# First two token tiles of a two-layer transformer kernel: centred only, with the deviation applied to the logits

## The chip, the cores and the metric

The kernel runs on one core of one Trainium2 chip. A core has a TensorE for matrix products (PE in the profile, with PEld for its weight loads), a VectorE (DVE), a ScalarE (ACT) and a GpSimd (POOL), each with its own in-order instruction queue, and a SyncE (SP) whose queue issues the DMAs here. The metric is the device time of one execution in microseconds. Four executions of the kernel before took 1617.11 to 1617.64 us, median 1617.24.

## The reference

The input x has 2048 tokens of 1024 numbers in bf16. Two kinds of layer alternate, two of each, all with the same weights:

```python
x = x + _A_ref(_layernorm(x, axis=-1), A_wqkv, A_wo)
x = x + _B_ref(_layernorm(x, axis=-1), B_w1, B_w3, B_w2)
x = x + _A_ref(_layernorm(x, axis=-1), A_wqkv, A_wo)
x = x + _B_ref(_layernorm(x, axis=-1), B_w1, B_w3, B_w2)
```

`_layernorm` is (x - mean) / sqrt(var + 1e-5) without gain or bias. `_A_ref` is an attention of 32 heads of 32 numbers over a window: token s looks at the eight tokens s, s-2, ..., s-14. The logit of a head is q · k * 32^-0.5, positions before the first token are masked, a softmax over the eight follows, and the weighted sum of v goes through `wo`. `_B_ref` is a gated feed-forward: silu(x w1) * (x w3), 3584 wide, times w2.

Since a layer norm's division is one number per token, and q is linear in the normalised token, the division can as well be made on the token's logits: with q computed from (x - mean) alone, q · k has to be multiplied by 1/sqrt(var + 1e-5) of the query's token before mask and softmax.

## The kernel before, in words

**Tiling.** A token tile is 128 tokens (x_sb[0] to x_sb[15], all kept in SBUF), a chunk is four tiles (512 tokens). `ln` makes the layer norm of one chunk: per tile bn_stats on two halves, aggregate, root on ScalarE (L313), reciprocal (L315), subtract and multiply (L320) into a bf16 tile xn[j], and then a transpose into xnT, where the model dimension lies on the partitions in eight blocks of 128 (index kk). There are two xnT buffers, used by the stages in turn. For all chunks but the first the transpose is a DMA issued by SP (L253).

**Stages.** A q stage computes q, k and v of one chunk (24 groups of eight 128x512 products, L355), copies each result out of PSUM on ScalarE (L407; for chunk 0 k and v also straight into kT and vT, L410), and spills pairs of blocks to DRAM (qkv_d). An attention step works on half a chunk: load qT, kT, vT, multiply and add on VectorE (L259), transpose the partial sums so that tokens lie on partitions, sum to the logits L, mask, softmax (exp on ScalarE, L519), weighted sum, and the projection with `wo` on TensorE (32 products), added to x on VectorE (L545). A feed-forward stage runs two chains of products, silu on ScalarE (L568), the product on VectorE (L570), and a second run of products added to x (L600).

**What sets the order.** The kernel writes its operations down with reads, writes and an estimated duration. `Program.place` then plans one order for each engine's queue from these estimates, with classes as priorities (smaller goes first) and, for TensorE, lanes: lane 2 (the start's transposes) before lane 1 (the projections) before lane 0. The queues are executed in this order on the chip; nothing is reordered there. So a change at the start also shifts, by a group of products here and there, what stands where later on. A DMA is issued only after the DMA eight places before it has landed (the waits on eight completion semaphores in turn).

**The first stage.** `q_first` (L422) is special, because nothing can be computed until x has come in. SP issues x tiles 0 and 1 (256 KB each), then the q weights as eight rows kk of 256 KB, then x tiles 2 and 3 (L423 to L425), then the k weights in two pieces of 1 MB, x of chunk 1, and so on. Meanwhile TensorE multiplies a tile of zeros (`warm`, NWARM = 12 products of 128x512, L278). `ln(0, first=True)` handles tile after tile: statistics, root, apply, eight TensorE transposes into one PSUM bank (L334) and one ScalarE copy of 128x1024 into xnT (L339). The q products of chunk 0 (L438) have 128 columns, one token tile at a time, 8 output blocks m for each kk, in the order tile 0 kk 0 to 4, tile 1 kk 0 to 4, both kk 5 to 7, tile 2, tile 3:

```python
order = [(0, 0, 5), (1, 0, 5), (0, 5, 8), (1, 5, 8), (2, 0, 8), (3, 0, 8)]
```

Their results go by ScalarE (L444) to hT[:, 0:8], a buffer that the feed-forward stages need only later, and from there to DRAM. Then come k and v of chunk 0 (L355 from `q_tile`), and the attention of chunk 0 begins when q has been read back.

Of the kernel before, what the change touches and what calls it, by code (L numbers as in the profile page):

```python
# [154 lines left out]
def kernel(  # L155
# [24 lines left out]
    scale = float(Dh) ** -0.5  # L180
    EPS = 1e-5
    NSLOT = 6
    NWARM = 12

    xin = A_x[0].rearrange("(n p) d -> p n d", p=P)
    xout = out[0].rearrange("(n p) d -> p n d", p=P)
# [11 lines left out]
    def alloc(name, shape, dt=BF16):  # L198
        return sb.tile(shape, dt, name=name)
# [29 lines left out]
    rs = alloc("rs", [P, NE], FP32)  # L229
    rsb = alloc("rsb", [P, NE])  # L230
    An = alloc("An", [P, W, NE])
    oT = [alloc(f"oT{i}", [P, KT, TCH]) for i in range(2)]
    qkv_d = [[dram.tile([D, S], BF16, name=f"qkv_d{l}_{i}") for i in range(3)] for l in range(2)]
    bank = [pp.tile([P, 512], FP32, name=f"bank{i}") for i in range(8)]
# [6 lines left out]
    def t1(n):  # L241
        return 0.15 + n / 960.0

    def dve(dur, emit, reads, writes, cls=2, **kw):
        return pr.add("DVE", dur, emit, reads, writes, cls, **kw)
# [4 lines left out]
    def dma(kb, dst, src, reads, writes, cls=3, transpose=False):  # L250
        def emit(op):
            if transpose:
                nc.sync.dma_start_transpose(dst, src)  # L253
            else:
                nc.sync.dma_start(dst, src)
        return pr.add("SP", 0.45, emit, reads, writes, cls, size=kb * 1024)
# [28 lines left out]
    def take_slot():  # L285
        i = n_slot[0] % NSLOT
        n_slot[0] += 1
        return i

    def load_x(c, j0=0, j1=TPC, after=()):  # L290
        for j in range(j0, j1):
            n = c * TPC + j
            dma(256, x_sb[n][:], xin[:, n, :], after, [("x", n, 0), ("x", n, 1)], 0 if c == 0 else 3)
# [3 lines left out]
    def ln(c, first=False):  # L297
        s = stage_no[0]
        b, q = s % 2, s % 4
        xb = xnT[b]  # L300

        def stats(j):
            n = c * TPC + j
            pri = j - 9 if first else 1
            for hh in range(2):
                dve(0.67, lambda _, hh=hh: nc.vector.bn_stats(st[q][:, j, hh, :],  # L306
                                                              x_sb[n][:, hh * 512:(hh + 1) * 512]),
                    [("x", n, hh)], [("st", q, j, hh)], pri)
            dve(0.2, lambda _: nc.vector.bn_aggr(mv[q][:, j, :], st[q][:, j, :, :]),  # L309
                [("st", q, j, 0), ("st", q, j, 1)], [("mv", q, j)], pri)  # L310

        def root(j0, j1):
            act(0.3, lambda _: nc.scalar.activation(sd[q][:, j0:j1], mv[q][:, j0:j1, 1], ACTF.Sqrt, bias=epst[:]),  # L313
                [("mv", q, j) for j in range(j0, j1)] + ["eps"], [("sd", q, j) for j in range(j0, j1)], j0 - 9 if first else 0, table="sqrt")
            dve(0.16, lambda _: nc.vector.reciprocal(rstd[q][:, j0:j1], sd[q][:, j0:j1]),  # L315
                [("sd", q, j) for j in range(j0, j1)], [("rstd", q, j) for j in range(j0, j1)], j0 - 9 if first else 0)

        def apply(j):
            n = c * TPC + j
            dve(0.5, lambda _: nc.vector.tensor_scalar(xn[j][:], x_sb[n][:], mv[q][:, j, 0:1], rstd[q][:, j:j + 1],  # L320
                                                       op0=ALU.subtract, op1=ALU.mult),
                [("x", n, 0), ("x", n, 1), ("mv", q, j), ("rstd", q, j)], [("xn", j)], j - 9 if first else 1)

        if first:
            for j in range(TPC):
                stats(j)
                root(j, j + 1)
                apply(j)
                a = Acc()

                def tr(op, j=j, a=a):
                    pt = bank[a.bank][:].bitcast(BF16)
                    for kk in range(KT):
                        nc.tensor.transpose(pt[:, kk * P:(kk + 1) * P], xn[j][:, kk * P:(kk + 1) * P], ident[:])  # L334
                tro = pr.add("PE", 0.5, tr, [("xn", j), "ident"], [], takes=[a], lag=0.17, lane=2)

                def ev(op, j=j, a=a):
                    pt = bank[a.bank][:].bitcast(BF16)
                    nc.scalar.copy(xb[:, :, j * P:(j + 1) * P], pt.rearrange("p (k t) -> p k t", k=KT))  # L339
                evac(act, 1.0, ev, tro, [], [("xnT", b, j)], a)  # L340
            return b
        for j in range(TPC):
            stats(j)
        root(0, TPC)
        for j in range(TPC):
            apply(j)
            dma(256, xb[:, :, j * P:(j + 1) * P], xn[j][:], [("xn", j)], [("xnT", b, j)], 0, transpose=True)
        return b
# [10 lines left out]
    def evac(add, dur, emit, last_mm, reads, writes, a, cls=0, **kw):  # L359
        op = add(dur, emit, reads, writes, cls, gives=[a], **kw)  # L360
        op.deps.add(last_mm)
        return op

    wslots = {}

    def q_weights(which, split):
        ids = [take_slot(), take_slot()]
        for h, i in enumerate(ids):
            if split != "c":
                v = slot[i][:].rearrange("p (k c) -> p k c", k=4)  # L370
                for k in range(0, 4, 1 if split == "k" else 4):
                    n = 1 if split == "k" else 4
                    dma(256 * n, v[:, k:k + n, :], wqkv_v[:, 4 * h + k:4 * h + k + n, which * D:(which + 1) * D], [],
                        [("w", i, k + z) for z in range(n)], 0 if split == "k" else 3)
            else:
                v = slot[i][:].rearrange("p (k c) -> p k c", k=KT)
                dma(1024, v, wqkv_v[:, :, which * D + h * 512:which * D + (h + 1) * 512], [],
                    [("w", i, k) for k in range(4)], 3)
        return ids, split
# [35 lines left out]
    def q_stage(l, c):  # L415
# [3 lines left out]
            q_tile(l, c, which, ws, b)  # L419
        stage_no[0] += 1  # L420

    def q_first():  # L422
        load_x(0, 0, 2)  # L423
        wslots[0] = q_weights(0, "k")
        load_x(0, 2, 4)  # L425
        b = ln(0, first=True)
        accs = {}
        order = [(0, 0, 5), (1, 0, 5), (0, 5, 8), (1, 5, 8), (2, 0, 8), (3, 0, 8)]
        for j, k0, k1 in order:
            if j not in accs:  # L430
                accs[j] = [Acc(), Acc()]
            pa = accs[j]
            for kk in range(k0, k1):
                lk = [q_lhs(wslots[0], kk, m) for m in range(KT)]

                def emit(op, kk=kk, j=j, pa=pa, lk=lk):
                    for m in range(KT):
                        nc.tensor.matmul(bank[pa[m // 4].bank][:, (m % 4) * P:(m % 4 + 1) * P], lhsT=lk[m][0],  # L438
                                         rhs=xnT[b][:, kk, j * P:(j + 1) * P], start=(kk == 0 and m % 4 == 0),
                                         stop=(kk == KT - 1), skip_group_check=True)  # L440
                op = pr.add("PE", 8 * 0.056, emit, [lk[0][1], ("xnT", b, j)], [], takes=pa, lag=0.17)
            if k1 == KT:
                for g in range(2):
                    evac(act, 0.59, lambda _, a=pa[g], g=g, j=j: nc.scalar.copy(  # L444
                        hT[:, 4 * g:4 * g + 4, j * P:(j + 1) * P],
                        bank[a.bank][:].rearrange("p (m t) -> p m t", m=4)), op, [],
                        [("hT", 4 * g + m, j) for m in range(4)], pa[g])
        for m0 in range(0, KT, 2):
            dma(256, spill_view(0, 0, m0, 0), hT[:, m0:m0 + 2, :],
                [("hT", m, j) for m in (m0, m0 + 1) for j in range(TPC)], [("d", 0, 0, 0, m0)], 1)  # L450
        wslots[1] = q_weights(1, "s")
        load_x(1)
        load_x(2, 0, 2)
        wslots[2] = q_weights(2, "s")
        load_x(2, 2, 4, [("hT", 7, TPC - 1)])
        load_x(3, 0, 4, [("hT", 7, TPC - 1)])
        for which, key, tile_ in ((1, "kT", kT), (2, "vT", vT)):
            dve(0.11, lambda _, tile_=tile_: nc.vector.memset(tile_[:, :, 0:HALO], 0.0), [], [(key, "h")], 1)
            q_tile(0, 0, which, wslots[which], b, (key, tile_))
        dma(2048, wo[:], wo_v, [("d", 0, 2, 0, 6)], ["wo"], 3)  # L460
        stage_no[0] += 1
# [25 lines left out]
    def t_stage(l, half):  # L487
# [22 lines left out]
                                                psm[:].rearrange("p w s -> p (w s)")), allA, ["pB"])  # L510
        dve(1.22, vtt(l2, psmT[:, :, 0:2], psmT[:, :, 2:4], ALU.add), ["pB"], [l2k])
        dve(t1(512), vtt(L.rearrange("p w e -> p (w e)"), l2[:, :, 0], l2[:, :, 1], ALU.add), [l2k], [Lk])
        if tok0 == 0:
            dve(t1(64), vtt(L[:, :, 0:8], L[:, :, 0:8], maskT[:], ALU.add), [Lk, "mask"], [Lk])
        dve(t1(256), vtt(m4, L[:, 0:4, :], L[:, 4:8, :], ALU.max), [Lk], [Lk])
# [157 lines left out]
```

## Time and profile before

| | us |
|---|---|
| the profiled execution, whole | 1617.13 |
| its span (first to last instruction) | 1615.4 |
| TensorE busy | 1602.9 |
| VectorE busy | 1120.5 |
| ScalarE busy | 329.0 |
| GpSimd busy | 1.9 |
| HBM traffic over the span | 166 GB/s |

The profile is of one execution. Its page has the busy time of each engine, the span in 40 slices, the DMA queues, the chain of work that ended last, the costliest groups of instructions by line, and the DMA issues. The trace can be asked for more: a timeline (start and duration of each instruction or run of equal instructions, with the idle time before it and what ended it in brackets), and for a DMA the time from issue to landing. Line numbers in the profile are those of the kernel. A TensorE group's duration includes the tail of its last product, so groups that follow each other overlap by some 0.2 us. SPq rows are the times that SP spends on issuing, not the transfers. In a row `out<-in` names the tiles, with buffer numbers left out; `x8` is the number of instructions run together.

### The profile page before, as it was taken

How to read it: one execution, taken by the hardware profiler on the slowest of the kernel's cores; microseconds unless marked ns; L12 is line 12 of the kernel's file. 1: busy time of each engine (PE TensorE's matmuls, PEld its weight loads, DVE VectorE, ACT ScalarE, POOL GpSimd, SP SyncE). 2: the span in 40 equal slices, each digit the busy share in tenths (PEclk: the TensorE clock that was granted, in tenths of full speed). 3: DMA queues.
4: the chain of work that ended last, by engine and by line, in shares of the span. 5: the costliest groups of instructions: out<-in, count | busy, mean ns of one | idle time of the engine just before them, and what ended most of it. 6: DMA issues, size and time to landing. Idle time of an engine off the chain costs nothing.

```text
span 1615.4 us, 19247 instructions
## 1 busy us (share of the span) xinstructions
PE 1602.9 (99%) x7569; PEld 764.7 (47%) x7716; DVE 1120.5 (69%) x1900; ACT 329.0 (20%) x519; POOL 1.9 (0%) x12
## 2 busy tenths in 40 slices
PE   9999999999999999999999999999999999999999
PEld 7555544444444444444444444444444444444444
DVE  5898888889889888888898728884298832211211
ACT  4423322021211222113211032110321101101110
POOL 0000000000000000000000000000000000000000
PEclk9999999999999999999999999999999999999999
DMA  9734755385548663858545487465873464454451
GB/s 313 216 106 140 234 170 158 121 225 177 171 132 242 198 199 125 219 166 247 176 142 157 162 245 224 127 169 178 251 226 118 156 183 156 144 173 153 156 165 44
DMA packets 347818, 285.30 MB, mean 177 GB/s; under 512 B 70096, under 2 KB 342480, under 8 KB 347600
## 3 DMA queue, kind: packets, MB, share of 16 engines
q1 hardware_dynamic: 347728, 284.07, 58.4%
q8 instruction: 60, 0.98, 0.3%
q14 instruction: 30, 0.25, 0.0%
HBM read 238.94 MB, written 29.36 MB: 166 GB/s over the span
## 4 chain that ended last, share of the span: by engine, by line
PE 99%; issue 0%; DVE 0%; DMA 0%; ACT 0%
PE bank L355 98%; PE bank L438 1%; DMA x<-in_A_x_dram 0%; DVE st L306 0%; PE bank L334 0%; ACT xnT L339 0%; DVE xn L320 0%; DVE x L600 0%; DVE mv L309 0%; DVE rstd L315 0%
## 5 line engine op out<-in xcount | busy, mean ns | idle before, releaser
L355 PE MATMUL bank<-xnT,slot 128*128 128x512 bf16 x4955 | 1088.7, 379 | 5.3
L355 PEld LDWEIGHTS <-slot 128*128 128x128 bf16 x5056 | 518.0, 102 | 573.0
L355 PE MATMUL bank<-slot,hT 128*128 128x512 bf16 (+2 forms) x1812 | 387.3, 372 | 1.9
L570 DVE TENSOR_TENSOR hT<-sg,bank 128x512 bf16<-128x512 bf16 x224 | 153.5, 685 | 212.4 <-PE bank L355 196.0
L259 DVE TENSOR_TENSOR scr<-scr 128x1024 bf16<-128x1024 bf16 (+3 forms) x576 | 293.7, 540 | 2.1
L355 PEld LDWEIGHTS <-hT 128*128 128x128 bf16 x1848 | 178.6, 98 | 208.7
L568 ACT ACTIVATE sg<-bank 128x512 bf16<-128x512 f32 x224 | 133.7, 597 | 654.1 <-PE bank L355 611.1
L259 DVE TENSOR_TENSOR scr<-qT,kT 128x2048 bf16<-128x2048 bf16 x128 | 154.3, 1222 | 70.3 <-DMA kT<-qkv_d 70.3
L407 ACT CAST sgt<-bank 128x512 bf16<-128x512 f32 x184 | 107.5, 585 | 290.2 <-PE bank L355 276.6
L259 DVE TENSOR_TENSOR scr<-pA,vT 128x2048 bf16<-128x2048 bf16 x128 | 152.9, 1222 | 0.4
L600 DVE TENSOR_TENSOR x<-x,bank 128x512 bf16<-128x512 bf16 (+1 forms) x66 | 43.7, 670 | 122.6 <-PE bank L355 122.4
L355 PE MATMUL bank<-wo,oT 128*128 128x512 bf16 x502 | 112.6, 379 | 0.5
L306 DVE BATCH_NORM_STATS2 st<-x 128x6 f32<-128x512 bf16 x128 | 84.3, 682 | 18.6 <-DMA x<-in_A_x_dram 18.1
L355 PEld LDWEIGHTS <-oT 128*128 128x128 bf16 x512 | 50.1, 98 | 60.3
L545 DVE TENSOR_TENSOR x<-x,bank 128x512 bf16<-128x512 bf16 x64 | 43.9, 686 | 35.9 <-PE bank L355 34.4
L313 ACT ACTIVATE sd<-mv,epst 128x4 f32<-128x4 f32 (+1 forms) x19 | 5.7, 298 | 189.1 <-DVE mv L309 189.1
L509 DVE STREAM_TRANSPOSE pB<-pA 128x2048 bf16<-128x2048 bf16 x16 | 37.0, 2310 | 0.4
L528 DVE STREAM_TRANSPOSE pA<-pB 128x2048 bf16<-128x2048 bf16 x16 | 37.0, 2309 | 0.4
L320 DVE TENSOR_SCALAR xn<-x,mv,rstd 128x1024 bf16<-128x1024 bf16 x64 | 31.6, 542 | 6.8 <-DMA xnT<-xn 6.6
L259 DVE TENSOR_TENSOR pA<-scr 128x256 bf16<-128x256 bf16 x128 | 35.9, 288 | 0.3
L568 ACT ACT_TABLE_LOAD x20 | 25.7, 1283 | 51.0 <-PE bank L355 50.8
L259 DVE TENSOR_TENSOR oT<-scr 128x256 bf16<-128x256 bf16 x128 | 34.2, 289 | 0.1
(41 smaller groups left out, 202.0 us busy)
## 6 DMA issues: line engine op xcount, KB each, us to landing
slot<-in_B_w_dram SPq DMA_DIRECT2D x160, 1024.0 KB, 5.8
slot<-in_A_wqkv_dram SPq DMA_DIRECT2D x28, 1024.0 KB, 5.3
qkv_d<-sgt SPq DMA_DIRECT2D x92, 256.0 KB, 4.1
qT<-qkv_d SPq DMA_DIRECT2D x16, 512.0 KB, 5.7
slot<-in_B_w_dram SPq DMA_DIRECT2D x16, 512.0 KB, 5.4
kT<-qkv_d SPq DMA_DIRECT2D x14, 544.0 KB, 6.8
vT<-qkv_d SPq DMA_DIRECT2D x14, 544.0 KB, 5.6
x<-in_A_x_dram SPq DMA_DIRECT2D x16, 256.0 KB, 4.9
```

The costliest lines, as they stand in the source:

```text
L259: return lambda _: nc.vector.tensor_tensor(o, a, b, op=op)
L306: dve(0.67, lambda _, hh=hh: nc.vector.bn_stats(st[q][:, j, hh, :], x_sb[n][:, hh * 512:(hh + 1) * 512]), [("x", n, hh)], [("st", q, j, hh ...
L320: dve(0.5, lambda _: nc.vector.tensor_scalar(xn[j][:], x_sb[n][:], mv[q][:, j, 0:1], rstd[q][:, j:j + 1], op0=ALU.subtract, op1=ALU.mult), ...
L355: nc.tensor.matmul(bank[a.bank][:, 0:ncol], lhsT=w, rhs=r, start=first and i == 0, stop=last and i == n - 1)
L407: evac(act, 0.59, lambda _, a=a, i=i, m=m: nc.scalar.copy(sgt[i][:, m % 2, :], bank[a.bank][:]), op, [], [("sgt", i, m % 2)], a)
L438: nc.tensor.matmul(bank[pa[m // 4].bank][:, (m % 4) * P:(m % 4 + 1) * P], lhsT=lk[m][0], rhs=xnT[b][:, kk, j * P:(j + 1) * P], start=(kk = ...
L509: dve(2.31, lambda _: nc.vector.transpose(psmT[:].rearrange("p c d -> p (c d)"), psm[:].rearrange("p w s -> p (w s)")), allA, ["pB"])
L528: dve(2.31, lambda _: nc.vector.transpose(At[:].rearrange("p w s -> p (w s)"), AeT[:].rearrange("p c d -> p (c d)")), ["pB"], allA)
L545: evac(dve, t1(512), lambda _, xs=xs, a=a: nc.vector.tensor_tensor(xs, xs, bank[a.bank][:], op=ALU.add), op, [("x", n, hh)], [("x", n, hh) ...
L568: evac(act, 0.6, lambda _, i=i, a=ag: nc.scalar.activation(sg[i][:], bank[a.bank][:], ACTF.Silu), og, [], [("sg", i)], ag, table="silu")
L570: evac(dve, t1(512), lambda _, i=i, a=au, f=f: nc.vector.tensor_tensor(hT[:, f, :], sg[i][:], bank[a.bank][:], op=ALU.mult), ou, [("sg", i ...
L600: evac(dve, t1(cn), lambda _, xs=xs, a=a, cn=cn: nc.vector.tensor_tensor(xs, xs, bank[a.bank][:, 0:cn], op=ALU.add), op, [("x", n, hh)], [ ...
```

## The change

For token tiles 0 and 1 of chunk 0 the q products no longer take the normalised token, but the centred one, x - mean:

- x tile 0 is loaded as two halves. Its sum is made in two halves, one on VectorE and one on ScalarE, both with an accumulating output; the sum of tile 1 is made on ScalarE in one instruction. The mean of tile 0 is a small VectorE instruction over the two partial sums.
- `tensor_scalar` subtracts the mean from the tile. The result is transposed on TensorE, and the copy out of PSUM is split: blocks 0 to 3 on VectorE, 4 to 7 on ScalarE, into a part of hT called `ce`.
- The q weights' rows 0 to 2 are loaded before x tiles 2 and 3, rows 3 to 7 after them. The q products of tiles 0 and 1 have 128 columns for kk 0 to 2 (tile 0, then tile 1) and 256 columns (both tiles) for kk 3 to 7, into four PSUM banks; those of tiles 2 and 3 have 256 columns throughout, one bank after another. The 256 products of 128 columns become 48 of 128 and 104 of 256.
- Tiles 2 and 3 are normalised as before and transposed on TensorE. Tiles 0 and 1 are normalised after them, for k and v only, and transposed into xnT by two DMAs on SP's queue, which stand in front of the loads of x chunk 1.
- Sixteen small GpSimd copies lay out the two tiles' 1/sqrt(var + eps) for the logits: 32 partitions by 2 numbers each, from one group of 32 partitions to another, into rsx. In the first attention step of the first layer one VectorE multiplication of 128x512 numbers in fp32 scales the logits by it, ahead of the mask.
- NWARM is 10 and not 12. In `ln` the priorities at the start are one number and not one per tile.

```diff
-    NWARM = 12
+    NWARM = 10
...
-        def stats(j):
+        def stats(j, after=()):
...
+    def transposed(src, key, dst, dkeys, both):
+        a = Acc()
+
+        def tr(op):
+            pt = bank[a.bank][:].bitcast(BF16)
+            for kk in range(KT):
+                nc.tensor.transpose(pt[:, kk * P:(kk + 1) * P], src[:, kk * P:(kk + 1) * P], ident[:])
+        tro = pr.add("PE", 0.5, tr, [key, "ident"], [], takes=[a], lag=0.17, lane=2)
...
+        if both:
+            ev(dve, nc.vector.tensor_copy, 0, 4, 0.68)
+            ev(act, nc.scalar.copy, 4, 8, 0.59)
+        else:
+            ev(act, nc.scalar.copy, 0, 8, 1.0)
+
     def q_first():
-        load_x(0, 0, 2)
-        wslots[0] = q_weights(0, "k")
+        for hh in range(2):
+            dma(128, x_sb[0][:, hh * 512:(hh + 1) * 512], xin[:, 0, hh * 512:(hh + 1) * 512], [], [("x", 0, hh)], 0)
+        load_x(0, 1, 2)
+        rows = q_weights(0, "k", load=False)
+        wslots[0] = rows[:2]
+        for kk in range(3):
+            rows[2](kk)
         load_x(0, 2, 4)
-        b = ln(0, first=True)
...
+        for kk in range(3, KT):
+            rows[2](kk)
+        b, q, stats, root, apply = ln(0, first=True)
+        ce = hT[:, 8:16, :]
+        dve(0.45, lambda _: nc.vector.tensor_scalar(xn[2][:, 0:512], x_sb[0][:, 0:512], 0.0, 0.0, op0=ALU.add,
+                                                    op1=ALU.add, accum_out=part[:, 0:1]),
+            [("x", 0, 0)], [("xn", 2), ("part", 0)], -9)
+        act(0.75, lambda _: nc.scalar.activation(xn[3][:, 0:512], x_sb[0][:, 512:1024], ACTF.Copy,
+                                                 accum_out=part[:, 1:2]), [("x", 0, 1)], [("xn", 3), ("part", 1)], -9)
+        dve(0.16, lambda _: nc.vector.tensor_scalar(mean[:, 0:1], part[:, 0:1], part[:, 1:2], 1.0 / D, op0=ALU.add,
+                                                    op1=ALU.mult), [("part", 0), ("part", 1)], [("mean", 0)], -9)
+        act(1.15, lambda _: nc.scalar.activation(xn[3][:], x_sb[1][:], ACTF.Copy, scale=1.0 / D,
+                                                 accum_out=mean[:, 1:2]), [("x", 1, 0), ("x", 1, 1)],
+            [("xn", 3), ("mean", 1)], -9)
+        for j in range(2):
+            dve(0.5, lambda _, j=j: nc.vector.tensor_scalar(xn[j][:], x_sb[j][:], mean[:, j:j + 1], None,
+                                                            op0=ALU.subtract),
+                [("x", j, 0), ("x", j, 1), ("mean", j)], [("xn", j)], -9)
+            transposed(xn[j], ("xn", j), ce[:, :, j * P:(j + 1) * P], [("ce", j, k) for k in range(KT)], True)
+        for j in range(2, TPC):
+            stats(j)
+            root(j, j + 1)
+            apply(j)
+            transposed(xn[j], ("xn", j), xnT[b][:, :, j * P:(j + 1) * P], [("xnT", b, j)] * KT, False)
+        for j in range(2):
+            stats(j, [("xn", TPC - 1)])
+            root(j, j + 1)
+            apply(j)
+            dma(256, xnT[b][:, :, j * P:(j + 1) * P], xn[j][:], [("xn", j)], [("xnT", b, j)], 0, transpose=True)
+        for g in range(4):
+            for n in range(4):
+                pr.add("POOL", 0.2, lambda _, g=g, n=n: nc.gpsimd.tensor_copy(
+                    rsx[32 * g:32 * (g + 1), :].rearrange("i (j n) -> i j n", n=4)[:, :, n],
+                    rstd[q][32 * n:32 * (n + 1), 0:2]), [("rstd", q, 0), ("rstd", q, 1)], [("rsx", g)])
...
+        pa = [Acc() for _ in range(4)]
+        for kk, j0, j1 in [(k, j, j + 1) for j in range(2) for k in range(3)] + [(k, 0, 2) for k in range(3, KT)]:
...
+                    nc.tensor.matmul(bank[pa[m // 2].bank][:, t0 + j0 * P:t0 + j1 * P], lhsT=lk[m][0],
+                                     rhs=ce[:, kk, j0 * P:j1 * P], start=(kk == 0 and m % 2 == 0 and j0 == 0),
+                                     stop=(kk == KT - 1), skip_group_check=True)
...
+                        nc.tensor.matmul(bank[pa[g].bank][:, m * 2 * P:(m + 1) * 2 * P], lhsT=lk[m][kk],
+                                         rhs=xnT[b][:, kk, 2 * P:4 * P], start=(kk == 0 and m == 0),
+                                         stop=(kk == KT - 1), skip_group_check=True)
...
         wslots[1] = q_weights(1, "s")
-        load_x(1)
-        load_x(2, 0, 2)
-        wslots[2] = q_weights(2, "s")
+        load_x(1, 0, 4, [("xn", 1)])
+        load_x(2, 0, 2, [("xn", 1)])
+        wslots[2] = q_weights(2, "s", after=[("xn", 1)])
...
+        if l == 0 and tok0 == 0:
+            Lb = L.rearrange("p w (n h) -> p w n h", h=8)
+            dve(t1(512), vtt(Lb, Lb, rsx[:].unsqueeze(1).unsqueeze(3).to_broadcast([P, W, NB, 8]), ALU.mult),
+                [Lk] + [("rsx", g) for g in range(4)], [Lk])
         if tok0 == 0:
```

## The prediction

> **What bounds the kernel now.** I read the page's busy shares and its chain of waits first, then the timeline of the first 45 us engine by engine, then the places further on where TensorE's input comes from VectorE or from a transposing DMA.
>
> From the page, busy shares and the chain that ended last:
>
> ```profile
> span 1615.4 us, 19247 instructions
> PE 1602.9 (99%) x7569; PEld 764.7 (47%) x7716; DVE 1120.5 (69%) x1900; ACT 329.0 (20%) x519; POOL 1.9 (0%) x12
> PE 99%; issue 0%; DVE 0%; DMA 0%; ACT 0%
> ```
>
> TensorE is the bound. Its stretch of 128x512 products (L355) starts at 24.01 and ends at 1612.63. The program holds 7360 products of that size in it (the four-piece tail counted by columns), and 1588.62 us / 7360 = 0.2158 us each; 49 of them take 10.74 us in the chain, so there is no stall in these 1588 us. Whatever the change is worth is therefore the shift of 24.01, plus any stall that it creates later.
>
> The timeline up to 24 us (start, duration, engine, line, what):
>
> ```profile
> 1.19 5.30 PE L278 MATMUL bank<-warm 128*128 128x512 bf16 x12 [1.19 <-DVE warm L274]
> ...
> 3.40 1.88 DVE L306 BATCH_NORM_STATS2 st<-x 128x6 f32<-128x512 bf16 x3 [2.12 <-DMA x<-in_A_x_dram]
> ...
> 6.10 0.49 DVE L320 TENSOR_SCALAR xn<-x,mv,rstd 128x1024 bf16<-128x1024 bf16 x1
> ...
> 6.66 1.32 PE L334 MATMUL bank<-ident,xn 128*128 128x128 bf16 x16 [0.17 <-DVE xn L320]
> ...
> 7.54 1.93 ACT L339 COPY xnT<-bank 128x1024 bf16<-128x1024 bf16 x2 [1.02 <-PE bank L334]
> ...
> 8.60 6.41 PE L438 MATMUL bank<-xnT,slot 128*128 128x128 bf16 x112 [0.63 <-ACT xnT L339]
> ...
> 11.42 1.88 DVE L306 BATCH_NORM_STATS2 st<-x 128x6 f32<-128x512 bf16 x3 [4.12 <-DMA x<-in_A_x_dram]
> ...
> 24.01 21.32 PE L355 MATMUL bank<-xnT,slot 128*128 128x512 bf16 x97
> ```
>
> Statistics, normalising, transposing and copying tile 0 keep the real products back until 8.60; from there TensorE is dense. 6.41/112 = 0.057 us per 128-column product. 8.60 to 24.01 is 15.41 us: 256 products and 16 transposes.
>
> Two places where a later stage could stall. The last x tile transposed by DMA before the first feed-forward stage (time to landing in the second line), and the first output projection with its VectorE input:
>
> ```profile
> 185.69 1.29 SPq L253 DMA_TRANSPOSE xnT<-xn  x1
> xnT<-xn SPq DMA_TRANSPOSE x1, 3.1
> ...
> 102.84 0.50 DVE L259 TENSOR_TENSOR oT<-scr 128x256 bf16<-128x256 bf16 x2
> 106.67 1.67 PE L355 MATMUL bank<-wo,oT 128*128 128x512 bf16 x7
> ```
>
> That transpose lands at 188.8; the stage starts at 24.01 + 768 x 0.2158 = 189.8, 1.0 us later. The projection finds its input 3.3 us old.
>
> **The change, step by step.** I call K the start of the k projection (24.01 before).
>
> *Centring instead of normalising.* Removed ahead of tile 0: two bn_stats, aggregate, root, reciprocal (3.40 to 6.10). Added: x tile 0 in two DMAs, half a sum on VectorE, half on ScalarE, one tiny add, one subtract. The whole tile is there by 3.40; the second half is issued one slot (0.87/2 = 0.43 us) later, so 3.4 to 3.85, I take 3.6. ScalarE's half sum: the nearest row is its 128x512 copy, 0.585, plus a read of the accumulator that no row shows: 0 to 0.3 (a 128x1 root takes 0.295); I take 0.15, giving 4.35. The add like a 128x1 reciprocal (0.16) and a hop of 0.09 (8.51 to 8.60): 4.6. Subtract 0.49: 5.2 (4.9 to 5.6). VectorE's own half sum runs beside ScalarE's. TensorE however is busy with ten dummy products of 0.427 (5.30 is twelve with the last one's tail): 1.19 + 4.27 = 5.46. The transposes start at 5.55 (5.46 to 5.7), against 6.66.
>
> *Transposes and the copy out of PSUM.* 6.66 to 7.54 is 0.88, kept (up to 1.06, should all eight take a quarter of the dummies' 0.427 and then the tail of 0.2). The copy is now two halves, 4 blocks on ScalarE and 4 on VectorE. In the changed program's order VectorE's half waits for ScalarE's, and for tile 1 it is the other way round, so they follow each other: ScalarE 0.58 (its 512-element rows), hop 0.09, VectorE 0.6 (no row: between 0.42 for 128x512 in bf16 and 0.69 for the PSUM addition), hop 0.09. First product at 5.55 + 0.88 + 1.36 = 7.8 (7.5 to 8.3), 0.8 us before the old 8.60. Side by side it would be 7.15.
>
> The Trainium skill speaks against the halves ("PSUM — Partial Sum Buffer", section "PSUM bank collisions raise a hardware error"): two engines must not read one bank in the same partitions at once, so the split buys no overlap; no run here shows a collision. By that rule the sum is mine; with overlap it would be 1615.5.
>
> *Products.* 48 of 128 columns (2.75), 104 of 256, 16 transposes of tiles 2 and 3 (0.92). No row has 256 columns: between 0.1079 (half of 0.2158) and 0.114 (twice 0.057); on the line through both sizes 0.110, so 11.45 (11.2 to 11.9). Sum 15.1 against 15.41: 0.3 saved.
>
> *Waits inside.* The weight rows landed from 6.06 (issue 1.66 + 4.4) to about 10.8, then x2 and x3 to 12.0: 0.66 us per 256 KB. Now x2, x3 stand after row 2. Rows 0 to 2 land by 7.7, rows 3 to 7 from about 9.7 to 12.3; they are wanted at 7.8, 10.6 and no faster than every 0.88 us after, so no wait. x2 is there at about 8.4 and, with the 3.2 us from 11.42 to its normalised tile at 14.61, gives xn2 at 11.6 and xn3 at 12.3; TensorE reaches their transposes at 13.2. ScalarE copies both (0.97 each) while rows 6 and 7 run: at most 0.1 us is lost. K = 7.8 + 15.1 + 0.1 = 23.0.
>
> *Tiles 0 and 1 for k and v.* They are normalised after tile 3 on VectorE (four bn_stats of 0.65, done near 15) and carried by two DMA transposes. Their roots stand behind ScalarE's copy of tile 3 (about 15.8), tile 1's also behind a q store that waits for the last row-7 product: its apply ends near 17.7. The transposes are issued at 17.0 and 18.4 (1.3 us of SP each) and land 3.1 to 6.7 after issue, median 3.4 over all 60. The 1 MB k loads before them drain near 17.5 (2 MB at 0.385 MB/us after 12.2), so I take 3.4: 21.8, 1.2 us before K. Hidden.
>
> *What SP holds back.* SP sits waiting for tile 0 from about 8.5 to 17; the loads of x4 onward go out at 19.7 and not at 8.76. Cover: chunk 1's last transpose landed at 37.5 and is wanted at K + 27.6 = 50.6. The v weights go out near 23 to 24.5 and land near 32; wanted at K + 13.8 = 36.8.
>
> *GpSimd and the logits.* 16 copies on POOL (its 32x64 select takes 0.28): 2 to 8 us from 17.7, first read near 75. One 128x512 f32 multiplication on VectorE, 0.69, in the first attention alone; about 1.7 us more of it also stands behind the wait for chunk 2's transposes. The projection's input moves from 103.3 to about 105, and TensorE comes for it eight products later in its order, at K + 84.6 = 107.6. Hidden by 2.6 us.
>
> *The first feed-forward stage.* The second projection also stands eight products later, so the root comes at K + 155.9 instead of K + 154.2. But the two 1 MB loads in front of the transposes are issued 6 us earlier, and the four transposes stand together: 4 x 1.38 and a landing, as at 51.6, end at K + 164.5; wanted at K + 165.8. Hidden by 1.2 us.
>
> **Sum.** 0.8 + 0.3 - 0.1 = 1.0 us off the span: 1614.4. The profiled execution took 1617.13, 1.73 more than its span, and lies 0.11 under the median of 1617.24. Forecast 1616.1; I write 1616.2, since two of the hops are the shortest seen.
>
> The clock: the dummies take 0.427 and the products 0.057 for a quarter of the columns, half the time, while the granted clock reads 1.00 throughout; TensorE doubled its rate near 7 us. Now it idles from about 6.9 to 7.8. The skill ("TensorE: Matmul & The Clock Gate", "What's actually happening") says that a free-running window of about 3.4 us must be busy before the rate doubles; a window more at half rate would cost an estimated 1.7 us, 1617.9.
>
> **Rivals.**
> 1. *The transposes of tiles 0 and 1 land after q is done* (slower than before). For it: under the early load landings of 6.2, 5.4 and 4.1 were seen at 27.7 to 31.4. Against: the queue should be drained. It costs from 4.6 us of landing on and makes the kernel slower than before from 5.6 on; at 6.7, K = 25.1: 1618.2.
> 2. *The first feed-forward stage waits.* With transposes as slow as before (9.7 us from first issue to last landing) they end at K + 166.8: 1.0 us lost, 1617.1.
> 3. *No head start*: sums and serial copies eat it (half sums of 0.9, dummies in the way) and the first product stays near 8.5: 1616.8.
> 4. *TensorE stays at half rate.* For it: the idle stretch before 7.8. 48 products at 0.057 more are 2.7 us (1618.9); all of q would be 13.6 us (1629.8).
>
> **How the numbers follow.** Forecast (1615.5 to 1616.7) 0.60, rival 1 0.11, rival 2 0.08, rival 3 0.11, rival 4 0.05, a stall that I don't see further on 0.05. The range 1615.2 to 1618.3 holds the forecast, rivals 2 and 3 and rival 1. 0.2% is 3.2 us, about what a measurement of this kernel can tell from no change. Nothing here gains that (the first product can't come before 7.2): 0.02 faster. Slower by that much needs half of rival 4 or a hidden stall: 0.08. The rest, 0.90, is within.
>
> **What would show it.** Right: first real product at 7.5 to 8.3, k projection at 22.5 to 23.7, no idle TensorE after it. Wrong: ScalarE and VectorE copying halves at the same time; an idle stretch in front of the k projection released by the transposes; 128-column products still 0.1 us apart after 9 us; a gap near 189.

## The result, and the profile after

| | before | after |
|---|---|---|
| median of the runs, us | 1617.35 (61 runs, 1616.86 to 1619.42) | 1616.02 (41 runs, 1615.12 to 1617.16) |
| the profiled execution, us | 1617.13 | 1615.99 |
| its span, us | 1615.4 | 1614.2 |
| first real product of q at, us | 8.60 | 7.05 |
| k projection begins (K) at, us (first record) | 24.01 | 22.42 |

The changed kernel takes 0.9991 of the time before, with a 95% interval of 0.9987 to 0.9995: 1.3 us less. In a second set of runs on one chip it took 1616.05 (11 runs) against 1617.29. The forecast was 1616.2.

From the page of the changed kernel, busy shares and the chain that ended last:

```profile
span 1614.2 us, 19065 instructions
PE 1601.0 (99%) x7463; PEld 762.7 (47%) x7610; DVE 1123.7 (70%) x1908; ACT 326.7 (20%) x521; POOL 5.0 (0%) x28
PE 99%; issue 1%; DMA 0%; SPq 0%; DVE 0%
```

GpSimd works 3.1 us more and VectorE 3.2 us more than before; GpSimd doesn't stand in the chain, and VectorE only with the last addition to x, 0.29 us behind the last product. From 22.42 on TensorE has no idle stretch. So, as before, the whole difference is made ahead of K. The timeline of the start (start, duration, engine, line, what):

```profile
1.19 3.89 PE L281 MATMUL bank<-warm 128*128 128x512 bf16 x10 [1.19 <-DVE warm L277]
...
3.41 0.63 ACT L449 ACTIVATE xn<-x 128x512 bf16<-128x512 bf16 x1 [1.19 <-DMA x<-in_A_x_dram]
3.95 0.19 ACT L449 ACTIVATION_READ_ACCUMULATOR xn<-x 128x1 f32 x1
...
4.42 0.49 DVE L457 TENSOR_SCALAR xn<-x,mean 128x1024 bf16<-128x1024 bf16 x1
...
4.96 0.62 PE L419 MATMUL bank<-ident,xn 128*128 128x128 bf16 x8
5.93 0.56 ACT L425 COPY hT<-bank 128x512 bf16<-128x512 bf16 x1
...
6.52 0.43 DVE L425 COPY hT<-bank 128x512 bf16<-128x512 bf16 x1
...
7.05 2.84 PE L490 MATMUL bank<-hT,slot 128*128 128x128 bf16 x48
10.16 2.79 PE L490 MATMUL bank<-hT,slot 128*128 128x256 bf16 x24 [0.26 <-DMA slot<-in_A_wqkv_dram]
...
15.43 7.15 PE L504 MATMUL bank<-xnT,slot 128*128 128x256 bf16 x64
16.36 2.88 SPq L256 DMA_TRANSPOSE xnT<-xn  x2
16.49 3.65 POOL L473 COPY rsx<-rstd 32x2 f32<-32x2 f32 x16 [13.72 <-DVE rstd L318]
22.42 3.83 PE L342 MATMUL bank<-xnT,slot 128*128 128x512 bf16 x16
```

The reader is to see three things. The centred tile is ready at 4.9, the normalised one was at 6.6. ScalarE's half of the copy ends at 6.49 and VectorE's begins at 6.52: they follow each other. And at 10.16 TensorE has been idle for weight row 3, which the prediction did not have. The chain of waits says the same of that row: it is issued at 4.50 and lands at 10.11.

```profile
4.50 5.61 DMA slot<-in_A_wqkv_dram
10.11 0.05 issue
10.16 2.79 PE bank L490 x24
```

A word on reading K. In the chain of the kernel before, the stream of 128x512 products comes in pieces:

```profile
24.01 10.74 PE bank L355 x49
...
34.80 10.74 PE bank L355 x49
```

A piece has 49 products, and the next begins 10.79 us later, which is 50 products of 0.2158: the record of every fiftieth product is missing. The missing one stands just ahead of a piece, and ahead of 24.01 it is the first k product: the weight loads of the stream begin at 23.73, and the product itself must have begun at 23.79. So 0.22 of the 1.59 by which K moved is a missing record, and K really moved by 1.37 us. The last product's end says the same: 1612.63 before, 1611.26 after. Each product is drawn some 0.16 longer than its distance to the next one, so a stop inside the stream costs its drawn idle and some 0.16 more.

The two later places:

```profile
102.52 0.51 DVE L262 TENSOR_TENSOR oT<-scr 128x256 bf16<-128x256 bf16 x2
...
107.02 5.34 PE L342 MATMUL bank<-wo,oT 128*128 128x512 bf16 x23
...
179.49 5.44 SPq L256 DMA_TRANSPOSE xnT<-xn  x4
```

The projection's input is ready 4.0 us before TensorE comes for it. The last of the four transposes lands 3.15 us after its issue at 183.65, at 186.8; the stage wants it at K + 165.8 = 188.2.

### The profile page after: what moved, and what is told of

It reads as the page before. It is cut to its first block, busy times and chain, and to the rows that moved or that the text cites. A ratio compares the mean times of both kernels' runs of the same rounds, so it can differ in the third digit from the quotient of the medians.

```text
span 1614.2 us, 19065 instructions
## 1 busy us (share of the span) xinstructions
PE 1601.0 (99%) x7463; PEld 762.7 (47%) x7610; DVE 1123.7 (70%) x1908; ACT 326.7 (20%) x521; POOL 5.0 (0%) x28
## 4 chain that ended last, share of the span: by engine, by line
PE 99%; issue 1%; DMA 0%; SPq 0%; DVE 0%
PE bank L342 98%; PE bank L504 0%; DMA slot<-in_A_wqkv_dram 0%; PE bank L490 0%; SPq L258 0%; PE bank L419 0%; DVE x L667 0%
```

## The experiments

The theory at the outset: time follows K, and K follows the first product and, behind it, the landing of weight row 3. All numbers in one table; the kernel before was run beside each on the same chip, and first product, K and span are of one profiled execution.

| kernel | median us (lowest to highest) | before beside it | first product | K | span |
|---|---|---|---|---|---|
| after_again | 1616.05 (1615.41 to 1616.49) | 1617.29 | 7.62 | 22.54 | 1614.3 |
| a1_normed | 1620.21 (1617.58 to 1620.89) | 1617.70 | 9.27 | 25.82 | 1617.5 |
| a1b_normed_act | 1617.28 (1616.54 to 1618.58) | 1617.39 | 8.22 | 23.14 | 1614.8 |
| a2_onecopy | 1616.03 (1615.38 to 1616.40) | 1617.70 | 7.59 | 22.51 | 1614.2 |
| a3_twobanks | 1615.80 (1615.20 to 1617.95) | 1617.70 | 7.10 | 22.46 | 1614.2 |
| a4_loadsfirst | 1626.81 (1626.26 to 1627.64) | 1617.70 | 7.59 | 31.27 | 1625.8 |
| b1_row3 | 1616.67 (1616.05 to 1617.80) | 1617.39 | 6.75 | 22.54 | 1614.3 |
| b3_warm8 | 1615.90 (1615.38 to 1617.30) | 1617.39 | 6.99 | 22.42 | 1614.1 |
| b5_nologits | 1616.05 (1615.51 to 1616.44) | 1617.29 | 7.26 | 22.18 | 1613.9 |
| c1_best | 1617.50 (1616.51 to 1618.80) | 1617.39 | 6.84 | 21.77 | 1615.5 |
| c5_replan | 1615.43 (1615.12 to 1615.92) | 1617.29 | 6.75 | 21.89 | 1613.6 |

**Is it the centring?** First the tiles normalised ahead again, the rest of the change kept:

```diff
-        for j in range(2):
-            dve(0.5, lambda _, j=j: nc.vector.tensor_scalar(xn[j][:], x_sb[j][:], mean[:, j:j + 1], None, ...
-            transposed(xn[j], ("xn", j), ce[:, :, j * P:(j + 1) * P], ..., True)
-        for j in range(2, TPC):
+        for j in range(TPC):
             stats(j)
             root(j, j + 1)
             apply(j)
-            transposed(xn[j], ("xn", j), xnT[b][:, :, j * P:(j + 1) * P], ..., False)
+            transposed(xn[j], ("xn", j), xnT[b][:, :, j * P:(j + 1) * P], ..., j < 2)
```

> The changed kernel with tiles 0 and 1 normalised (statistics, root, apply) ahead of their q products, as before the change; the row order of the weights, the 256-column products, the split copies and ten dummies stay; no centring, no DMA transposes at the start, no scaled logits. Theory (centring buys the earlier first product, and time follows K, the start of the k projection): first product near 8.4 instead of 7.05, K 23.4 to 24.3 instead of 22.42, time 1617.0 to 1617.9, that is 0.4 below to 0.5 above the kernel before. Rival (the gain comes from wider products and the order of the loads): K near 22.5, time near 1616.1.

K came 1.5 us later than the highest of these values, at 25.82, and the median is 4.2 us above the changed kernel's. The timeline of TensorE in this kernel, and under it the granted clock by stretch (from:to, length, TensorE busy, clock, DMA share, GB/s):

```profile
1.18 4.45 PE L281 MATMUL bank<-warm 128*128 128x512 bf16 x10 [1.18 <-DVE warm L277]
6.62 1.32 PE L419 MATMUL bank<-ident,xn 128*128 128x128 bf16 x16 [0.99 <-DVE xn L323]
9.27 5.34 PE L464 MATMUL bank<-xnT,slot 128*128 128x128 bf16 x56 [1.33 <-DVE xnT L425]
```

```profile
6.60:8.00 1.40, 1.24 (x16) 1.00 1.04 378
9.20:11.00 1.80, 1.73 (x19) 0.60 1.05 403
11.00:13.00 2.00, 2.00 (x22) 0.51 1.05 396
13.00:15.00 2.00, 2.00 (x31) 1.00 1.06 392
```

Two things went wrong that have nothing to do with normalising. VectorE's copy of its half stands behind the statistics of tile 2 in VectorE's queue, and these wait for tile 2's load until 8.20; so the copy comes at 8.81 and the first product at 9.27. And after 1.33 us of idleness the granted clock falls to one half until 13.0: the 56 products take 5.34 us, where the next kernel needs 3.71 for the same number. This is the half rate that rival 4 of the prediction feared, as a fall after the dummies. The experiment doesn't measure centring.

So once more, with ScalarE alone copying (nothing behind the statistics) and twelve dummies (no idle TensorE):

```diff
-    NWARM = 10
+    NWARM = 12
...
-            transposed(xn[j], ("xn", j), xnT[b][:, :, j * P:(j + 1) * P], ..., j < 2)
+            transposed(xn[j], ("xn", j), xnT[b][:, :, j * P:(j + 1) * P], ..., False)
```

> Tiles 0 and 1 are normalised ahead of q again (no centring, no scaling of the logits, no transposing DMAs); TensorE gets its twelve dummies back, so that it isn't idle before the first product, and ScalarE alone copies out of PSUM, so that no copy stands behind VectorE's statistics of tile 2. The row order and the 256-column products of the change stay. Theory (centring gives the earlier start): first product 8.4 to 8.7, K 23.5 to 24.0, time 1617.0 to 1617.6, that is 1.0 to 1.6 above the changed kernel. Rival (what was gained comes from the larger products and the row order, and centring is worth nothing because weight row 3 holds q back anyway): K 22.4 to 22.8, time 1616.0 to 1616.4.

1617.28, within the theory's bounds, and 0.9991 to 1.0009 of the kernel before. First product and K lie 0.2 and 0.4 under the theory's values, but this profiled execution was the fastest of the eleven: the K of 23.14 belongs to 1616.54. The first product at 8.22 is 0.6 to 1.2 later than with centring, and the rival, that row 3 would hold q back anyway, is out.

How much of the gain is the centring's is less clear. By the medians, with 256-column products and the new row order but without centring, no gain is left that these runs can tell from none. The profiled execution says less:

```profile
3.06 2.07 DVE L309 BATCH_NORM_STATS2 st<-x 128x6 f32<-128x512 bf16 x3 [1.78 <-DMA x<-in_A_x_dram]
8.22 3.71 PE L464 MATMUL bank<-xnT,slot 128*128 128x128 bf16 x56 [0.40 <-ACT xnT L425]
```

Tile 0 comes in halves here too, and its statistics begin at 3.06 and not at 3.40; the first product is 0.38 earlier than in the kernel before without any centring. With 0.27 from the products (8.22 to 23.14 is 14.92, against 15.19) that makes 0.65, and the last product ended at 1611.99, 0.64 earlier. Centring adds 0.6 to 0.7 in the two profiled executions of the changed kernel, which is half of the gain; by the medians it is all of it. What slowed the other ten executions of this kernel isn't known. The granted clock over the whole run reads 1.000 in all but the slowest, where the 3.4 us at half rate in a1_normed made it 0.999, so it wasn't such a fall.

**The split copy.** ScalarE copies whole tiles, or the halves lie in two PSUM banks:

In a2_onecopy:

```diff
-            transposed(xn[j], ("xn", j), ce[:, :, j * P:(j + 1) * P], ..., True)
+            transposed(xn[j], ("xn", j), ce[:, :, j * P:(j + 1) * P], ..., False)
```

In a3_twobanks, where `transposed` makes two groups of four transposes, each with a bank of its own:

```diff
-        a = Acc()
+        def part(k0, k1, add, fn, dur):
+            a = Acc()
...
-            ev(dve, nc.vector.tensor_copy, 0, 4, 0.68)
-            ev(act, nc.scalar.copy, 4, 8, 0.59)
+            part(0, 4, dve, nc.vector.tensor_copy, 0.43)
+            part(4, 8, act, nc.scalar.copy, 0.59)
```

> The changed kernel, but tiles 0 and 1 are copied out of PSUM by ScalarE alone in one instruction each. Theory (the two halves follow each other: 0.56 + 0.43 + two hops against 0.97 and one hop): first product within 0.15 of 7.05, K within 0.3 of 22.42, time within 0.4 of the changed kernel's. Rival (splitting the copy is worth half of it): first product 0.4 later, time 0.4 above.

> The changed kernel, but the two halves of tiles 0 and 1 are transposed into two PSUM banks, so that VectorE's copy need not wait for ScalarE's. Theory: the two copies run at the same time, the first product comes at about 6.5 (0.5 earlier), but K does not move (22.3 to 22.5), because the products then wait longer for weight row 3, which lands at 10.1; time within 0.3 of the changed kernel's. Rival (the first product sets K): K 0.5 earlier, time 0.5 below.

Neither can be told from the changed kernel. One ScalarE copy takes 1.02 us, the two halves with the hop between them 1.06 (6.52 to 7.58 in the repeated run of the changed kernel): in one bank the split buys nothing, as the prediction had it. The halves follow each other there because the kernel's order has them so; what two engines reading one bank at once would do, no run shows. With two banks VectorE's half, which the first products read, no longer waits for ScalarE's: it is copied from 6.11 on, ScalarE's from 6.53, and the first product comes at 7.10 (the theory had 6.5), right behind tile 1's transposes, although the ten dummies took 4.45. In c5_replan below, also with two banks, the halves of tile 0 run side by side: ScalarE's from 6.04 to 6.63, VectorE's from 6.15 to 6.57. The chain of waits of a3_twobanks shows where the gain went:

```profile
7.26 0.90 PE bank L490 x16
...
8.20 1.96 PE bank L490 x32
10.16 0.05 issue
10.21 2.79 PE bank L490 x24
```

TensorE waits for weight rows 2 and 3 instead, which land at 8.16 and 10.16: its products of these rows start at 8.20 and 10.21. K stays at 22.46, as the theory had it.

**What SP holds back.** The loads of x chunk 1 and of the v weights go out at once, not after tile 1's second normalising:

```diff
-        load_x(1, 0, 4, [("xn", 1)])
-        load_x(2, 0, 2, [("xn", 1)])
-        wslots[2] = q_weights(2, "s", after=[("xn", 1)])
+        load_x(1)
+        load_x(2, 0, 2)
+        wslots[2] = q_weights(2, "s")
```

> The changed kernel, but the loads of x chunk 1, of two tiles of chunk 2 and of the v weights do not wait for tile 1's apply, so they stand before the two DMA transposes in SP's queue. Theory (the transposes land in time only because SP holds these loads back): the second transpose lands at 25 to 30 instead of 21.1, TensorE idles in front of the k projection, K 25 to 30, time 1618.6 to 1623.6. Rival (the transposes have slack whatever stands before them): K 22.4, time 1616.0.

K = 31.27, 1626.81: slower than even this theory's highest value. SP issued the two transposes at 19.89 and 24.7 (it was 16.36 and 17.82), and they landed 9.6 and 6.5 us later (3.9 and 3.3 in the changed kernel). TensorE and its clock in this kernel:

```profile
31.27 14.01 PE L342 MATMUL bank<-xnT,slot 128*128 128x512 bf16 x51 [8.59 <-DMA xnT<-xn]
```

```profile
26.00:28.00 2.00, 0.00 (x0) 0.69 1.52 141
28.00:31.00 3.00, 0.00 (x0) 0.50 1.03 278
35.00:37.00 2.00, 2.00 (x6) 0.50 1.04 390
37.00:39.00 2.00, 2.00 (x11) 1.00 1.75 199
```

The span grew by 11.6: 8.85 is K, and the other 2.8 are the first 5.6 us of the stream at half the clock. Rival 1's mechanism is real; what prevents it in the changed kernel is that SP keeps the queue empty for the two transposes.

**Weight row 3 earlier.** One more q row ahead of x tiles 2 and 3:

```diff
-        for kk in range(3):
+        for kk in range(4):
             rows[2](kk)
         load_x(0, 2, 4)
-        for kk in range(3, KT):
+        for kk in range(4, KT):
```

> The changed kernel with rows 0 to 3 of the q weights ahead of x tiles 2 and 3 (before: rows 0 to 2). Theory (K is set by row 3's landing at 10.1, and behind it by the two copies of tiles 2 and 3 on ScalarE): no idle TensorE before the products of row 3, but tiles 2 and 3 come 0.66 us later, so that their copies end near 15.9; K 22.4 to 23.0, time 1616.0 to 1616.6. Rival (only row 3 matters): K 22.1, time 1615.7.

The wait for row 3 is gone, and another has taken its place, as the theory said: ScalarE copies tiles 2 and 3 one after the other until 15.51, and TensorE is idle for 0.69 us before 15.55. 1616.67 is 0.07 above the theory's range and no better than the changed kernel; the profiled execution, 1616.14, was one of the two fastest.

**The dummies.** Fewer of them:

```diff
-    NWARM = 10
+    NWARM = 8
```

> The changed kernel with eight dummy products and not ten. Theory (the dummies aren't on the path, as row 3's landing sets K): dummies end near 4.6 or earlier, first product 7.0 to 7.3, K 22.3 to 22.6, time 1615.8 to 1616.3. Rival (the dummies are what brings TensorE to its full rate, and after a break it falls back): 128-column products at 0.1 us each for some or all of the first 48, K 23.5 to 25.0, time 1617.1 to 1618.7, with a spread over the runs above 1.5 us.

1615.90; the first product at 6.99, no change in K. Three of its eleven runs took 1616.6 to 1617.3: the spread of 1.9 us is the rival's, time and K are the theory's. The granted clock of the three reads 1.000, so a fall as in a1_normed (0.999) isn't the cause. Only one execution was profiled, so whether TensorE doubled its rate late in those three is open.

**The logits.** No GpSimd copies and no multiplication:

```diff
-        for g in range(4):
-            for n in range(4):
-                pr.add("POOL", 0.2, lambda _, g=g, n=n: nc.gpsimd.tensor_copy(...
...
-        if l == 0 and tok0 == 0:
-            Lb = L.rearrange("p w (n h) -> p w n h", h=8)
-            dve(t1(512), vtt(Lb, Lb, rsx[:]...
```

> The changed kernel without the sixteen GpSimd copies and without the multiplication of the logits (the logits of the first 256 tokens stay unscaled in the first layer, so this kernel leaves that part of the computation out). Theory (both are hidden, the copies by some 55 us and the multiplication by 2.6 us before the projection): K 22.4 to 22.6, time 1615.8 to 1616.3. Rival (GpSimd's copies hold a port or a queue that VectorE or SP needs, or the 0.7 us of VectorE is on the path): 0.3 to 0.7 faster than the changed kernel, 1615.3 to 1615.7.

1616.05, the same as the changed kernel's 1616.05 beside it. K was 22.18 in its profiled execution, 0.22 below the theory's range, because row 3 landed at 9.2 there and the ScalarE copy began at 6.16; nothing in either depends on what was left out. Copies and multiplication are hidden. K stands 14.92 behind the first product here, as in after_again and a2_onecopy, where row 3 was in time as well. Where row 3 came late (the first execution of the changed kernel, a3_twobanks, b3_warm8), K stands 12.25 to 12.26 behind the start of that row's products. So K follows the later of the two, as the theory at the outset has it.

**Can the wait for row 3 and the copies' serial order both be taken away?** Row 3 early (as in b1_row3), and two banks (as in a3_twobanks) for all four tiles:

```diff
-        for kk in range(3):
+        for kk in range(4):
...
-            transposed(xn[j], ("xn", j), xnT[b][:, :, j * P:(j + 1) * P], ..., False)
+            transposed(xn[j], ("xn", j), xnT[b][:, :, j * P:(j + 1) * P], ..., True)
```

> Rows 0 to 3 ahead of x tiles 2 and 3, and each tile's eight transposes in two PSUM banks, one copied by VectorE and one by ScalarE, for all four tiles. Theory (halves in two banks are copied side by side, and row 3 no longer holds q back): first product 7.0 to 7.3, second half of q from 15.1 to 15.4, K 22.1 to 22.4, time 1615.6 to 1616.0. Rival (a weight row further on, or VectorE's statistics of tiles 0 and 1 standing ahead of its copies, takes the place): K 22.5 or more, time 1616.1 or more.

The start did as the theory said and more: second half of q at 14.78, K = 21.77, the earliest of all. Yet the kernel took 1617.50, and the rival's 1616.1 or more is met, though not its K, and not by any of the waits it named. TensorE's timeline further on:

```profile
37.43 12.74 PE L342 MATMUL bank<-xnT,slot 128*128 128x512 bf16 x58 [0.82 <-DMA slot<-in_A_wqkv_dram]
...
189.58 25.63 PE L342 MATMUL bank<-xnT,slot 128*128 128x512 bf16 x118 [0.85 <-DVE scr L262]
```

and SP's, at both places:

```profile
25.18 2.30 SPq L258 DMA_DIRECT2D qkv_d<-hT  x1
27.52 0.47 SPq L258 DMA_DIRECT2D slot<-in_A_wqkv_dram  x1
...
181.54 1.27 SPq L256 DMA_TRANSPOSE xnT<-xn  x1
182.90 0.53 SPq L258 DMA_DIRECT2D qkv_d<-sgt  x1
183.53 4.05 SPq L256 DMA_TRANSPOSE xnT<-xn  x3
```

The second half of the v weights stands behind a store that holds SP for 2.30 us, goes out at 27.52 (25.00 in the changed kernel) and lands at 37.4, wanted after 68 products, at 36.4. At 189.58 the profile names VectorE, but those products read xnT: the last transpose is issued at 186.3 and lands 3.2 us later, at 189.5. In this kernel's order the second projection stands 680 products behind K and not 672, and a store stands between the transposes. That is rival 2. With 0.16 for each stop: -0.65 + 0.98 + 1.01 = +1.34, and the span is 1.3 longer than the changed kernel's.

If this is right, the order alone is at fault. The same instructions, planned with another estimate for the second half of q:

```diff
-            ops.append(pr.add("PE", 16 * 0.1092, emit,
+            ops.append(pr.add("PE", 16 * 0.125, emit,
```

> The instructions of the kernel with row 3 early and two PSUM banks for all tiles, whose q started 0.6 us earlier but which lost 0.82 us at 36.6 (second half of the v weights) and 0.85 us at 188.7 (first feed-forward stage). Only an estimate of the planner is changed (16 products of 256 columns at 0.125 and not 0.1092 us each), which puts the first two projections back to 392 and 672 products after K (they were at 400 and 680), the two v loads next to each other, and the four transposes of the feed-forward stage without stores between them. Theory (the two stalls are all that was lost): K 21.7 to 22.0, no idle TensorE after, time 1615.3 to 1615.7. Rival (the v weights or something else still waits as q ends earlier): K 21.7 to 22.0 with an idle stretch, time 1616.0 or more.

> The changed kernel itself once more, so that the others of this call are compared with it on one chip: 1615.8 to 1616.3, K 22.3 to 22.9.

Both as the theory had it. From c5_replan's timeline:

```profile
6.75 6.55 PE L490 MATMUL bank<-hT,slot 128*128 128x128 bf16 x80
...
14.90 7.15 PE L504 MATMUL bank<-xnT,slot 128*128 128x256 bf16 x64
21.89 18.29 PE L342 MATMUL bank<-xnT,slot 128*128 128x512 bf16 x82
```

There is no idle stretch behind it. 1615.43 us is 0.6 under the changed kernel on the same chip and 1.9 under the kernel before (ratio 0.9988, interval 0.9980 to 0.9997); its slowest run (1615.92) is below the median of the changed kernel, of whose eleven runs beside it four are faster than that. It beats the kernel before, and by the medians the changed kernel too.

## Why the prediction was right, and where its terms were not

*The bound.* Right: nothing stalls behind K, and the last product's end moved by 1.37, as K did. Only 24.01 was not the start of the stream: that was 23.79, ahead of the first record.

*Head start, 0.8.* The working took the dummies at half rate to their end. The repeated run of the changed kernel is that case: dummies 4.45, then

```profile
5.63 0.87 PE bank L419 x8
6.50 0.02 issue
6.52 0.59 ACT hT L425
7.12 0.02 issue
7.14 0.44 DVE hT L425
7.58 0.04 issue
7.62 5.46 PE bank L490 x72
```

Transposes 0.87 (0.88 in the working), ScalarE's half 0.59 (0.58), VectorE's 0.44 (0.6), hops of 0.02 and 0.04 (0.09). The first product at 7.62 and not 7.8: the mis-sized terms are VectorE's half, taken between two rows when the lower one (0.42) was right, and the hops. In the other profiled execution of the changed kernel TensorE doubled its rate near 4.3 us, the dummies ended at 5.08, and the transposes began at 4.96, below the lower end of 5.46; the first product came at 7.05, ahead of the 7.2 that the prediction held to be the earliest possible. The term that failed there is the dummies' 0.427 each. By its rows ScalarE's copy began 0.35 after the transposes' end at 5.58, because ScalarE's sum of tile 1, ahead of it in the queue, ran to 5.93; the prediction had no such wait. And not all of the head start is the centring's: a1b_normed_act has 0.38 of it without.

*Sums.* ScalarE's half sum and its read of the accumulator, two rows that overlap, took 0.73 (3.41 to 4.14), on the estimate of 0.585 + 0.15; the second half of the tile was there at 3.41 and not at 3.6.

*Products, 0.3, and the wait inside, 0.1.* In the repeated run 7.62 to 22.54 is 14.92, against 15.19 from 8.60 to 23.79: 0.27 saved, as predicted, and no wait. Luck had a part in this: both sides of the prediction's difference were some 0.2 too high. Its 15.41 held the k product without a record, and its 15.1 had the tail of a row in the price of a product: without the tail they take 0.056 for 128 columns ((6.41 - 0.17)/112) and 0.109 for 256 ((7.15 - 0.17)/64), not 0.057 and 0.110. First product and products together: 0.98 + 0.27 = 1.25, and the last product ended 1.24 earlier (1611.39). In the first profiled execution the earlier start (1.55) met the sentence "so no wait": row 3 landed at 10.11 while TensorE had finished the first 48 products at 9.73, and some 0.4 went there. The predicted landing of 9.7 was wanted at 10.6; with the start 0.75 earlier and the landing 0.4 later the cover of 0.9 was gone. Row 3 landed between 9.2 and 10.2 in the executions seen, so it decides in some and not in others, and K comes out at 22.2 to 22.5 either way.

*K = 23.0.* Measured 22.42 and 22.54. Of the 0.46 to 22.54, some 0.2 is the first product, 0.2 the products, and 0.1 the wait that didn't come. The forecast of the time was nearer than that of K, 1616.2 against 1616.02, because the 24.01 of the kernel before was 0.2 too high as well. The gain was 1.33 where 1.04 was forecast (1617.24 less 1616.2); the difference is the first product, and the wait.

*Transposes of tiles 0 and 1.* Issued at 16.36 and 17.82 (17.0 and 18.4 predicted), the second lands at 21.1, 1.3 before K; the prediction had 1.2. Rival 1 did not come about; a4_loadsfirst shows its price.

*v weights.* "Land near 32" held for the first piece and not for the second: the two went out at 23.73 and 25.00 and landed 8.4 and 10.4 us later, at 32.1 and 35.4, the second wanted at 37.1. The slack is 1.7 us and not 4.8, and c1_best used it up.

*GpSimd, logits.* 3.65 us for the sixteen copies (2 to 8 predicted), 0.69 for the multiplication at 75.37. The projection's input at 103.0 (about 105), wanted at 107.0. Hidden, and b5_nologits confirms it.

*The first feed-forward stage.* Transposes end at K + 164.4 (K + 164.5 predicted), wanted at K + 165.8: hidden by 1.4. That this place decides next is shown by c1_best.

*The clock.* Rival 4 didn't come about in the changed kernel: the granted clock reads 1.00 through its idle stretches of 1.0 and 0.3 us. A fall is shown in a1_normed, where 1.33 us of idleness followed 1.0 us shortly before: the clock stayed down from about 9.5 to 13.0, 3.4 us. In a4_loadsfirst it was down from 26.8 to 37.0, 10.2 us, three times as long. The Trainium skill, "TensorE: Matmul & The Clock Gate", section "What's actually happening", has the rate decided by a free-running window of 3413 ns; the 3.4 us of a1_normed and the 10.2 us of a4_loadsfirst agree with that length. It also says that the array turns cold after at least one idle window; in a1_normed TensorE was without any instruction for less than 2 of the preceding 3.4 us and the clock fell nevertheless. But what it did in these 3.4 us was, but for the last 0.3, transposes, and no run here tells whether they keep the rate up as products do; so whether this goes against the page stays open.

## What to carry to other kernels

When one unit is dense from a certain point to the end, price a change at the start by that point alone, and then ask of each load and transpose behind it how much slack it has: here 1.4 and 1.7 us, and a start that was 0.65 us earlier, with what the planner made of it, used up both. Where a planner writes the queues from estimates, an improvement also re-sorts what comes later; compare the orders of the queues before blaming the improvement, since one estimate was worth 2 us. An experiment that undoes part of a change must leave the queues unblocked and TensorE busy, or it measures the block and the clock.

## What was not expected of the hardware

- The moment at which TensorE doubles its rate differs from execution to execution of the same start. Ten dummies took 3.9 us in two executions, 4.37 in one and 4.45 in seven; with 0.427 for a slow one, 0.2158 for a fast one and a tail of 0.2, the first means a change near 4.3 us, the last one after 5.6. The records show a granted clock of 1.00 during these slow dummies; the later falls (a1_normed, a4_loadsfirst) they do show, as 0.50.
- Centring needs the sum, and reading an accumulator is an instruction of its own: 0.19 us on ScalarE, 0.08 on VectorE.
- The DMA transpose of tile 0, 256 KB, landed 3.3 us after its issue with a quiet queue (after_again) and 9.6 us after it under the loads of a4_loadsfirst; SP's time for issuing two grew from 2.88 to 8.52 us.
- A GpSimd copy of 32x2 numbers from one group of 32 partitions to another took 0.23 us, 3.65 us for sixteen.
